# Closing the first expert list one unit earlier and moving the choices behind the unit's second scan

## The chip, the cores and the metric

The kernel runs on one core of a Trainium2 chip. The metric is device time in microseconds (us) of one execution, the median of several runs. Engines are named as in the profile: PE (matmuls), DVE (vector), ACT (scalar), POOL (indirect DMAs here), SP (the queue that issues most DMAs).

## What is computed

A gated recurrence over four sequences of 3648 steps, then a two-level mixture of experts over all 14592 rows. Cut to what matters:

```python
sig = 1.0 / (1.0 + np.exp(-f_logit))
f = lower_bound + (1.0 - lower_bound) * sig
for t in range(S):                                   # S = 3648, D = 256
    h = f[:, t] * h + (1.0 - f[:, t]) * x[:, t];  y[:, t] = h
x = y.reshape(B * S, D)                              # 14592 rows
g_idx = argmax(x @ w_group)                          # 4 groups
e_idx = argmax(x @ w_expert[g_idx])                  # 4 experts in each: 16 in all
out = g_w * e_w * (relu(x @ w1[g, e]) @ w2[g, e])    # w1 256x1024, w2 1024x256
```

The weights g_w and e_w are the two softmax values of the picked group and expert.

## The kernel before

**Phase one** walks over 29 units of 512 rows (the last has 256). For each unit it loads the gate and input (one 1 MB transfer `zt`), applies tanh and an affine map on ACT (L195, L205), multiplies on DVE (L241, later L221), runs two scans on DVE (L232, one for each half of the 256 features; the second is `p1_tb(u, 1)`), turns the result to row form with PE transposes (L259), computes router logits (L278, L291), and then **routes**: some thirteen small DVE instructions from `mx` (L301) to `posi` (L398) find each row's expert and its place in that expert's list; the count so far is kept in `runoff`, which ACT copies out of PSUM (L400). The rows are then scattered by POOL into the lists in HBM, one indirect DMA for each 128 rows (L361, `xs<-rows,posi`). Routing takes the units in groups: `GROUPS` says how many units are routed in one pass.

**Phase two** runs 32 jobs of two matrix products. Sixteen early jobs (A0 to A15) take the first 256 to 640 rows of a list before all rows are known; sixteen late ones (B0 to B15) take the rest in order of size, with at most `CAPS` rows each. `EARLY[i]` is, for early job i, the number of units after which its list is closed, and its length in 128-row tiles. `CHOOSE[i]` is the number of units after which its expert is picked, as the list that is fullest among those not yet taken (`choose`, L591 to L604 on DVE). A choice makes SP read the expert's number, write blank rows below the list, and start the expert's weight loads. When the list is closed, `place` (L615 to L622) fixes where the job's rows begin, and `early_rows` has SP load them (`xr<-xs`, L852), which waits for all scatters up to the cut. For A0 and A1 the weights are used as loaded, eight 256 KB pieces each (L867, matmuls L967 and L1002); later jobs load 512 KB pieces (L870) and split them on ACT and DVE (L878, L879).

The order on each engine is that of the code: phase one is a list of small steps (`p1_thunks`), and `bg_step` takes some of them after each step of phase two. `BEGIN` = 6 sets the mark "first": phase one runs alone up to it, then job A0 is entered. So PE, DVE and ACT each have one fixed sequence, with waits. Four `zt` buffers exist, so a unit's load waits until the unit four before it is scanned. SP's sequence is in code order too: a load that stands behind a wait on SP is issued after it.

In the code `u` is a unit number; in the step of unit u the unit u - 1 is routed. "After n units" is therefore the step u = n.

Of the kernel before, what the change touches and what calls it, by code (L numbers as in the profile page):

```python
# [19 lines left out]
NE = 16  # L20
UNIT = 512

EARLY = [(5, 2), (6, 2), (8, 2), (8, 2), (10, 3), (10, 3), (12, 3), (14, 3),
         (16, 4), (18, 4), (20, 4), (22, 5), (24, 5), (26, 5), (28, 5), (28, 5)]
CAPS = [972, 848, 808, 748, 536, 524, 516, 488, 448, 392, 340, 308, 240, 160, 144, 108]
EXTRA_AT = []
CHOOSE = [4, 5, 6, 6, 8, 8, 10, 12, 14, 16, 18, 20, 22, 24, 26, 26]
GROUPS = [1] * 6 + [2] * 11 + [1]
LAG = 7
FAST = 9  # L30
PLAN = []
ROWS_AT = {5: 6, 6: 7}
USED = float(1 << 22)
STG_BUFS = 8
RAW = 2
# [6 lines left out]
BEGIN = 6  # L42
# [6 lines left out]
def gated_scan_moe(ctx: ExitStack, tc, zx, lower, wroute, wexp, out, S):  # L49
# [7 lines left out]
    NT = N // P  # L57
    PRE = max(n for _, n in EARLY) * P
    LW = PRE + N + 2 * P
# [47 lines left out]
    nc.gpsimd.tensor_scalar(out=least, in0=eoff, scalar1=-16.0, scalar2=16.0, op0=ALU.mult, op1=ALU.add)  # L107
    cuts = {u for u, _ in EARLY}
    eidx = iota_f32("eidx", [NE], [[1, NE]])
# [297 lines left out]
    def p1_thunks(us, groups, parts):  # L407
# [21 lines left out]
        def put(f):  # L429
            th.append(f or (lambda: None))  # L430
            if hasattr(f, "mark"):
                marks[f.mark] = len(th)
# [11 lines left out]
        def wave(u, n):  # L444
            while parts and n and parts[0][0] <= u:
                put(parts.pop(0)[1])
                n -= 1
# [13 lines left out]
        for u in us + [us[-1] + 1]:  # L461
            seq = []
            if u <= FAST:
# [31 lines left out]
                elif u > 7:  # L495
                    wave(u, 1)
                    back(u - 1)
                for m in [m for m, v in ROWS_AT.items() if u == v]:
                    f = lambda m=m: early_rows(m)
                    f.mark = m  # L500
                    put(f)
                if u in cuts and u - 1 in ends:
                    put(lambda u=u: place(u))
                if u - 1 in ends:
                    put(lambda u=u: choose(u))
                put(lambda u=u: p1_tb(u, 1))
                wave(u, 1 if u < FAST else 99)
                if u == BEGIN:
                    f = lambda: None
                    f.mark = "first"  # L510
                    put(f)
                if u == FAST:
                    f = lambda: None
                    f.mark = "begun"
                    put(f)
                    for v in [v for v in sorted(cuts) if v <= FAST and v not in ROWS_AT]:
                        f = lambda v=v: early_rows(v)
# [16 lines left out]
            for t in seq:  # L534
                put(t)
                slot += 1
                for _ in range(1):
                    if not hold:
                        break
                    f = hold.popleft()  # L540
# [6 lines left out]
            if u - 1 in ends:  # L547
# [15 lines left out]
                if u in cuts:  # L563
                    rs.append(lambda u=u: place(u))
                    f = lambda u=u: early_rows(u)
# [10 lines left out]
        f = lambda: order()  # L576
# [673 lines left out]
```

## Time and profile before

| | |
|---|---|
| median of 3 runs | 781.66 us (780.29 to 782.87) |
| the profiled execution | 782.74 us |
| its span in the trace | 781.0 us |
| PE busy | 722.8 us (93%) |
| DVE busy | 536.1 us (69%) |
| ACT busy | 453.4 us (58%) |
| POOL busy | 293.5 us (38%) |

The span is what the instructions cover; the profiled execution's own time is 1.74 us longer. Busy shares are means over stages that differ, so the stages are read one by one.

### The profile page before, as it was taken

The page shows a single profiled execution, that of the slowest core. Times are in us where ns is not written, and L with a number is a line of the kernel's source. Part 1 is how long each engine was busy: PE and PEld are TensorE (multiplying, and loading weights), DVE is VectorE, ACT ScalarE, POOL GpSimd, SP SyncE. Part 2 cuts the span into 40 slices and gives each one's busy share as a digit, 9 for nine tenths or more (in the row PEclk, how much of TensorE's full clock was granted, in tenths as well). Part 3 has the DMA queues.
Part 4 walks back from the last instruction along what each step waited for, and adds up shares of the span by engine and source line. Part 5 has one row for each costly group of instructions (what it writes and reads, how often), then busy time and mean ns, then how long its engine had stood idle before and what let it go on. Part 6 is the DMA issues. An engine that isn't in the chain of part 4 may idle for free.

```text
span 781.0 us, 21520 instructions
## 1 busy us (share of the span) xinstructions
PE 722.8 (93%) x8182; PEld 641.8 (82%) x8182; DVE 536.1 (69%) x1154; ACT 453.4 (58%) x825; POOL 293.5 (38%) x272
## 2 busy tenths in 40 slices
PE   3666878999999999999999999999999999999995
PEld 1454657888888878998999989899999999999895
DVE  6885829999999996679456645554554656657661
ACT  5654827878878776454445544444454555556552
POOL 3641406858664764452221222222222231223222
PEclk9997979999999999999999999999999999999998
DMA  7798678998899875548857662334253555466530
GB/s 274 247 312 279 241 255 311 319 318 270 306 318 311 276 222 161 154 127 263 200 152 155 142 165 93 94 115 105 94 137 108 167 141 165 128 188 197 165 86 29
DMA packets 101963, 152.03 MB, mean 195 GB/s; under 512 B 60969, under 2 KB 70984, under 8 KB 98529
## 3 DMA queue, kind: packets, MB, share of 16 engines
q1 hardware_dynamic: 87328, 103.27, 46.5%
q0 software_dynamic: 11408, 30.02, 10.7%
q10 hardware_dynamic: 3120, 17.34, 6.4%
q8 instruction: 65, 1.06, 0.6%
q14 instruction: 42, 0.34, 0.2%
HBM read 112.66 MB, written 38.40 MB: 193 GB/s over the span
## 4 chain that ended last, share of the span: by engine, by line
PE 67%; DVE 16%; DMA 6%; issue 5%; ACT 3%; POOL 1%; SPq 1%; POOLq 0%; DVEq 0%; ACTq 0%
PE ps_m L1019 30%; PE ps_m L989 7%; PE ps_m L990 7%; PE ps_m L991 7%; DVE h L232 4%; DVE wl L879 3%; PE ps_p L989 3%; PE ps_p L990 3%; PE ps_p L991 3%; DVE hl L995 2%; DMA xs<-rows,posi 2%; PE ps_m L967 2%; PE ps_p L259 2%; DMA xr<-xs 2%; DMA xs<-blank 1%
## 5 line engine op out<-in xcount | busy, mean ns | idle before, releaser
L1019 PE MATMUL ps_m<-wh,hh 128*128 128x256 f16 (+3 forms) x1256 | 254.7, 251 | 1.2 <-ACT o L1031 1.2
L1019 PE MATMUL ps_m<-wh,hl 128*128 128x256 f16 (+3 forms) x1256 | 254.9, 251 | 0.1
L1019 PE MATMUL ps_m<-wl,hh 128*128 128x256 bf16 (+3 forms) x1256 | 254.7, 251 | 0.0
L1019 PEld LDWEIGHTS <-hh 128*128 128x128 f16 (+3 forms) x2512 | 186.3, 99 | 23.0 <-issue 4.5
L989 PE MATMUL ps_m<-xh,wh 128*128 128x256 f16 (+12 forms) x798 | 191.8, 255 | 6.0 <-DVE hl L995 5.5
L990 PE MATMUL ps_m<-xl,wh 128*128 128x256 bf16 (+12 forms) x798 | 192.0, 255 | 0.0
L991 PE MATMUL ps_m<-xh,wl 128*128 128x256 f16 (+12 forms) x798 | 191.9, 255 | 0.0
L879 DVE TENSOR_TENSOR wl<-st,wh 128x1024 bf16<-128x1024 f32 x120 | 144.7, 1218 | 57.3 <-ACT wh L878 57.3
L361 POOL DMA_INDIRECT xs<-rows,posi x114 | 139.3, 1222 | 116.5 <-ACT runoff L400 27.5
L1032 POOL DMA_INDIRECT out_dram<-o,info x71 | 82.9, 1167 | 235.2 <-ACT o L1031 203.2
L995 DVE SCALAR_TENSOR_TENSOR hl<-ps_m,hh 128x512 bf16<-128x512 f32 (+10 forms) x170 | 112.6, 666 | 61.2 <-ACT hh L994 60.9
L994 ACT ACTIVATE hh<-ps_m 128x512 f16<-128x512 f32 (+10 forms) x170 | 99.6, 589 | 66.8 <-PE ps_m L991 65.1
L878 ACT CAST wh<-st 128x1024 f16<-128x1024 f32 x120 | 124.3, 1049 | 14.1 <-PE ps_m L1019 8.7
L990 PEld LDWEIGHTS <-wh 128*128 128x128 f16 x1104 | 108.3, 98 | 12.9 <-issue 5.7
L989 PEld LDWEIGHTS <-wh 128*128 128x128 f16 x1104 | 108.2, 98 | 8.7 <-issue 1.0
L991 PEld LDWEIGHTS <-wl 128*128 128x128 bf16 x1104 | 108.2, 98 | 7.0
L1019 PEld LDWEIGHTS <-hl 128*128 128x128 bf16 (+3 forms) x1256 | 99.3, 99 | 10.0 <-issue 0.4
L1032 POOL DMA_INDIRECT out_dram<-o,meta x53 | 62.2, 1173 | 108.2 <-ACT o L1031 86.0
L1031 ACT ACTIVATE o<-ps_m,info 128x256 f32<-128x256 f32 (+4 forms) x71 | 31.5, 445 | 75.9 <-PE ps_m L1019 68.5
L989 PE MATMUL ps_p<-xh,wh 128*128 128x256 f16 (+17 forms) x306 | 71.5, 249 | 0.0
L991 PE MATMUL ps_p<-xh,wl 128*128 128x256 f16 (+17 forms) x306 | 71.4, 249 | 0.0
L990 PE MATMUL ps_p<-xl,wh 128*128 128x256 bf16 (+17 forms) x306 | 71.4, 249 | 0.0
(183 smaller groups left out, 840.7 us busy)
## 6 DMA issues: line engine op xcount, KB each, us to landing
st<-in_wexp_dram SPq DMA_DIRECT2D x120, 512.0 KB, 6.5
zt<-in_zx_dram ACTq DMA_DIRECT2D x16, 1024.0 KB, 8.4
zt<-in_zx_dram SPq DMA_DIRECT2D x10, 1024.0 KB, 10.1
xs<-blank SPq DMA_DIRECT2D x28, 258.0 KB, 10.0
xr<-xs SPq DMA_DIRECT2D x14, 258.0 KB, 4.1
wh<-in_wexp_dram SPq DMA_DIRECT2D x8, 256.0 KB, 5.8
wl<-in_wexp_dram SPq DMA_DIRECT2D x8, 256.0 KB
xs<-rows,posi POOLq DMA_INDIRECT x114, 6.1
```

The source lines that it names most:

```text
L232: nc.vector.tensor_tensor_scan(out=h[:, k, c0 - a:c1 - a], data0=ff[:, k, c0 - a:c1 - a], data1=uu[:, k, c0 - a:c1 - a], initial=init, op0 ...
L361: sc = nc.gpsimd.indirect_dma_start(out=xs_v[G["t0"] + t][:, :], out_offset=bass.IndirectOffsetOnAxis(ap=R["posi"][:, t:t + 1], axis=0), i ...
L878: nc.scalar.copy(j.wh[i], j.st[i])
L879: nc.vector.tensor_tensor(out=j.wl[i], in0=j.st[i], in1=j.wh[i], op=ALU.subtract)
L989: nc.tensor.matmul(po, w1_at(j.wh, k, c), xh[:, k], start=(k == 0), stop=False)
L990: nc.tensor.matmul(po, w1_at(j.wh, k, c), xl[:, k], start=False, stop=False)
L991: nc.tensor.matmul(po, w1_at(j.wl, k, c), xh[:, k], start=False, stop=(k == KD - 1))
L994: nc.scalar.activation(hi, pv, AF.Relu)
L995: nc.vector.scalar_tensor_tensor(out=j.hl[ch][:, cs[0]:cs[-1] + 1, 0:w], in0=pv, scalar=0.0, in1=hi, op0=ALU.max, op1=ALU.subtract)
L1019: nc.tensor.matmul(pm[i * q:i * q + n, 0:dw], h[ch][:, c, ts], w2_at(w, c)[:, i * dw:(i + 1) * dw], start=(c == 0 and s == 0), stop=(c == ...
L1031: nc.scalar.activation(o[s, 0:dw], pm[s, 0:dw], AF.Copy, scale=lt.bitcast(F32)[s, r, 1:2])
L1032: nc.gpsimd.indirect_dma_start(out=out_v[out_n[0]].rearrange("n (g d) -> (n g) d", g=g), out_offset=bass.IndirectOffsetOnAxis(ap=lt[s, r, ...
```

## The change

The first list is closed after four units (before: five) and its expert chosen after three (before: four); the second expert is chosen after four (before: five). The steps `place` and `choose` stand behind the unit's second scan (before: ahead of it), and the mark "first" ahead of that scan. Eight units are routed singly (before: six), then pairs. Job A0's rows are loaded in the step of unit 5 (before: 6), A1's in that of unit 7 as before. B0 may take 988 rows (before: 972).

```diff
-EARLY = [(5, 2), (6, 2), (8, 2), (8, 2), (10, 3), (10, 3), (12, 3), (14, 3),
+EARLY = [(4, 2), (6, 2), (8, 2), (8, 2), (10, 3), (10, 3), (12, 3), (14, 3),
-CAPS = [972, 848, 808, 748, 536, 524, 516, 488, 448, 392, 340, 308, 240, 160, 144, 108]
+CAPS = [988, 848, 808, 748, 536, 524, 516, 488, 448, 392, 340, 308, 240, 160, 144, 108]
-CHOOSE = [4, 5, 6, 6, 8, 8, 10, 12, 14, 16, 18, 20, 22, 24, 26, 26]
-GROUPS = [1] * 6 + [2] * 11 + [1]
+CHOOSE = [3, 4, 6, 6, 8, 8, 10, 12, 14, 16, 18, 20, 22, 24, 26, 26]
+GROUPS = [1] * 8 + [2] * 10 + [1]
-ROWS_AT = {5: 6, 6: 7}
+ROWS_AT = {4: 5, 6: 7}
...
+                if u == BEGIN:
+                    f = lambda: None
+                    f.mark = "first"
+                    put(f)
+                put(lambda u=u: p1_tb(u, 1))
+                wave(u, 1 if u < FAST else 99)
                 if u in cuts and u - 1 in ends:
                     put(lambda u=u: place(u))
                 if u - 1 in ends:
                     put(lambda u=u: choose(u))
-                put(lambda u=u: p1_tb(u, 1))
-                wave(u, 1 if u < FAST else 99)
-                if u == BEGIN:
-                    f = lambda: None
-                    f.mark = "first"
-                    put(f)
```

On DVE, the first choice of the kernel before stands between the end of a routing pass (`posi`) and the second scan of unit 4 (L232):

```order
L398 TENSOR_REDUCE posi<-sc 128x4
L591 SCALAR_TENSOR_TENSOR fill<-runoff,least 128x16
L593 MAX top<-fill 128x8
L595 MAX_INDEX who<-top,fill 128x8
L603 TENSOR_SCALAR sel<-fill,top 128x16
L604 SCALAR_TENSOR_TENSOR least<-sel,least 128x16
L232 SCALAR_TENSOR_TENSOR h<-zt,h 128x512
L241 SCALAR_TENSOR_TENSOR zt<-zt 128x1024
```

In the changed kernel the first choice comes one unit earlier, in the step of unit 3, and on DVE stands there as follows:

```order
L398 TENSOR_REDUCE posi<-sc 128x4
L232 SCALAR_TENSOR_TENSOR h<-zt,h 128x512
L591 SCALAR_TENSOR_TENSOR fill<-runoff,least 128x16
L593 MAX top<-fill 128x8
L595 MAX_INDEX who<-top,fill 128x8
L603 TENSOR_SCALAR sel<-fill,top 128x16
L604 SCALAR_TENSOR_TENSOR least<-sel,least 128x16
L241 SCALAR_TENSOR_TENSOR zt<-zt 128x1024
```

The scan has moved ahead of the choice, whose five rows now stand ahead of the next unit's multiplication (L241).

On SP, the start of the program (`zt` loads of whole units, then the first read of a chosen expert's number `who`), as a difference:

```order
 L183 DMA zt<-in_zx_dram 128x2x512 x2
-L185 DMA zt<-in_zx_dram 128x2048 x6
+L185 DMA zt<-in_zx_dram 128x2048 x5
 L597 TENSOR_LOAD who
 L597 ISA x2
```

One unit's load (that of unit 7) has moved behind the first choice and A0's eight weight loads. Likewise unit 8's load now stands behind A1's eight, and unit 9's behind A0's rows.

On DVE behind A0's entry, the kernel before routes units 6 and 7 in one pass of eight tiles (160 = 8 tiles of 20 logits), with a weight split (L879) between its rows:

```order
L232 SCALAR_TENSOR_TENSOR h<-zt,h 128x512 x2
L241 SCALAR_TENSOR_TENSOR zt<-zt 128x1024
L879 TENSOR_TENSOR wl_1238<-st,wh_1237 128x1024
L301 TENSOR_REDUCE mx<-Lg 128x40
L303 TENSOR_TENSOR ge<-Lg,mx 128x160
L232 SCALAR_TENSOR_TENSOR h<-zt,h 128x512
L307 SCALAR_TENSOR_TENSOR pw<-ge,pri 128x160
```

The changed kernel there has unit 8's multiplication and scans, and a pass for unit 6 alone; the pass for unit 7 begins behind unit 9's multiplication:

```order
L241 SCALAR_TENSOR_TENSOR zt<-zt 128x1024
L232 SCALAR_TENSOR_TENSOR h<-zt,h 128x512
L301 TENSOR_REDUCE mx<-Lg 128x20
L232 SCALAR_TENSOR_TENSOR h<-zt,h 128x512
L303 TENSOR_TENSOR ge<-Lg,mx 128x80
L307 SCALAR_TENSOR_TENSOR pw<-ge,pri 128x80
...
L398 TENSOR_REDUCE posi<-sc 128x4
L241 SCALAR_TENSOR_TENSOR zt<-zt 128x1024
L301 TENSOR_REDUCE mx<-Lg 128x20
```

One pass over eight tiles has become two passes over four, and the multiplication and two scans of unit 8, which stood ahead of A0's entry, stand behind it.

## Rows read from the trace of the kernel before

**Rows 1.** Busy time by stretch: PE, PEld, DVE, ACT, POOL, clock share, DMA share, GB/s.

```profile
40.00:44.00 4.00, 2.34 (x20) 1.62 (x21) 3.77 (x9) 2.50 (x6) 1.67 (x2) 1.00 0.76 139
44.00:64.00 20.00, 10.73 (x111) 8.97 (x109) 17.53 (x51) 8.89 (x20) 9.81 (x8) 0.95 1.03 377
...
66.00:75.00 9.00, 8.98 (x55) 6.09 (x56) 1.44 (x2) 5.21 (x12) 0.00 (x0) 0.66 0.73 210
...
103.00:113.00 10.00, 9.85 (x48) 7.60 (x48) 1.09 (x3) 2.08 (x5) 0.00 (x0) 0.67 0.79 252
...
140.00:300.00 160.00, 156.61 (x1648) 138.41 (x1646) 156.34 (x330) 126.34 (x239) 102.88 (x81) 1.00 0.89 288
300.00:781.00 481.00, 470.54 (x5809) 429.47 (x5806) 279.85 (x554) 243.18 (x419) 134.11 (x118) 0.99 0.52 140
```

**Rows 2.** PE in order of time: start, duration, work, idle before it and what ended that.

```profile
66.02 0.46 PE L933 MATMUL ps_p<-ident,xr 128*128 128x128 f32 x1 [8.02 <-DMA xr<-xs]
...
93.74 0.60 PE L967 MATMUL ps_m<-xl,wl 128*128 128x256 f32 x2
102.78 0.46 PE L933 MATMUL ps_p<-ident,xr 128*128 128x128 f32 x1 [8.44 <-DMA xr<-xs]
```

**Rows 3.** The chain of waits: start, duration, what.

```profile
50.92 7.25 DMA xs<-rows,posi
...
58.41 7.48 DMA xr<-xs
...
94.54 5.74 DMA xs<-rows,posi
...
101.18 2.17 DMA xr<-xs
```

**Rows 4.** DVE in order of time: a second scan, the first choice, a routing pass, the second choice.

```profile
29.49 1.27 DVE L232 TENSOR_TENSOR_SCAN h<-zt,h 128x512 f32<-128x512 f32 x1
...
37.68 0.17 DVE L591 SCALAR_TENSOR_TENSOR fill<-runoff,least 128x16 f32<-128x16 f32 x1 [1.66 <-ACT runoff L400]
...
38.18 0.17 DVE L595 FIND_INDEX8 who<-top,fill 128x8 uint32<-128x16 f32 x1
...
42.27 0.21 DVE L301 TENSOR_REDUCE mx<-Lg 128x20 f32<-128x80 f32 x1
...
44.95 0.22 DVE L398 TENSOR_REDUCE posi<-sc 128x4 int32<-128x64 f32 x1
46.76 0.18 DVE L615 SCALAR_TENSOR_TENSOR posA<-runoff,taken 128x16 int32<-128x16 f32 x1 [1.59 <-ACT runoff L400]
...
47.98 0.17 DVE L595 FIND_INDEX8 who<-top,fill 128x8 uint32<-128x16 f32 x1
```

**Rows 5.** ACT in order of time: the count of three units; unit 9's tanh.

```profile
30.96 0.18 ACT L400 COPY runoff<-ps_p 128x16 f32<-128x16 f32 x1
...
65.56 1.06 ACT L195 ACTIVATE zt<-zt 128x1024 f32<-128x1024 f32 x1 [7.42 <-DMA zt<-in_zx_dram]
```

**Rows 6.** SP's issues in order of time: loads of units 2 to 7, first blank, unit 9's load.

```profile
4.74 26.43 SPq L185 DMA_DIRECT2D zt<-in_zx_dram  x6
39.54 0.37 SPq L600 DMA_DIRECT2D xs<-blank  x1
...
55.72 0.80 SPq L185 DMA_DIRECT2D zt<-in_zx_dram  x1
```

**Rows 7.** DVE in order of time, later: four scans ahead of A0; units 6 and 7.

```profile
60.73 4.01 DVE L232 TENSOR_TENSOR_SCAN h<-zt,h 128x512 f32<-128x512 f32 x4
...
84.26 0.29 DVE L398 TENSOR_REDUCE posi<-sc 128x8 int32<-128x128 f32 x1
```

**Rows 8.** POOL: the first of the eight scatters of units 6 and 7.

```profile
85.32 0.97 POOL L361 DMA_INDIRECT xs<-rows,posi  x1 [22.53 <-ACT runoff L400]
```

**Rows 9.** PE at full rate: two following matmuls of 256 columns.

```profile
140.06 0.27 PE L990 MATMUL ps_m<-xl,wh 128*128 128x256 bf16 x1
140.17 0.27 PE L991 MATMUL ps_m<-xh,wl 128*128 128x256 f16 x1
```

## The prediction

> **What bounds the kernel now.** I read the busy time by stretch first, to split the run into stages, then the chain of waits for the start, then each engine in order of time around the gaps that the chain shows. From 140 us on PE is busy 156.6 of 160 us and then 470.5 of 481 [rows 1], and two matmuls of 256 columns follow each other at 0.11 us [rows 9], which is 2.4 GHz: nothing is to be won there by an earlier start of anything but the stage itself, and whatever arrives earlier at 140 us arrives earlier at the end. DVE is as full as PE up to 300 us (156.3 of 160), but its work behind A2's entry is the same in both kernels and in the same order, so it shifts too. The loss is ahead of that. PE does its first matmul for job A0 at 66.02, after 8.02 us of idle time; it runs out of A0 and A1 at 94.34 and waits 8.44 us for A2's rows, until 102.78 [rows 2]. Both times what ends the wait is a load of rows out of the lists, `xr`, which itself waits for the last scatter of the unit that closes the list: 50.92 to 58.17 to 65.89 for A0, 94.54 to 100.28 to 103.35 for the end of A2's loads [rows 3]. After both waits the clock stands at its lower level for a while: 0.66 over 66 to 75 and 0.67 over 103 to 113 [rows 1] mean about 6.1 and 6.6 us at 1.2 GHz.
>
> **The change: A0's start.** The first choice hangs on the count `runoff`. Before, DVE waits for it 1.66 us, then chooses; the number `who` is there at 38.35 [rows 4] and SP issues the blank rows at 39.54 [rows 6], the weights behind it. In the changed kernel the choice uses the count of three units, which ACT has at 31.14 [rows 5], and stands behind the scan that ends at 30.76 [rows 4]. With 0.1 us from the count to the choice and the same 0.67 to `who` as before (37.68 to 38.35 [rows 4]), `who` is there at 31.9: 6.5 us earlier. The five rows of a choice take about 1 us (0.67 and two more of some 0.2) and the wait behind the scan is some 0.5 us, so unit 4's multiplication and all behind it start 1.5 us later than before; this pushes unit 3's routing, but unit 4's second scan no longer waits for a count. The second choice, with a `place` ahead of it (46.76 to 48.15 for both until `who`), then ends at about 40.5 instead of 48.15: 7.6 us earlier.
>
> From the second `who` to A0's rows it took 17.7 us before (48.15 to 65.89). In it lie A1's eight weight pieces, one unit's `zt` (issued at 55.72) and the rows, while the DMA share is 1.03 at 377 GB/s [rows 1]. The same set follows the second choice now: eight pieces, then unit 8's `zt`, then A0's rows. The scatters that the rows wait for are one unit older: they come about 7.6 us earlier as well (the counts of two following units are 9.1 us apart, 37.68 against 46.76, less the 1.5 above), and they are not what lands last. So A0's rows land at 58.3 and PE starts there at 58.4. ACT's tanh ahead of A0's copies waits for unit 8's `zt` in place of unit 9's, which took 9.84 us from issue (55.72) to use (65.56) [rows 5, 6], so it moves along. **Term one: -7.6 us.** Its bounds: the first choice alone (-6.5) is inside; the 8.1 MB that flow from 40 to 64 us (139 GB/s for 4 us, 377 for 20 [rows 1]) would take 21.5 us at 377 GB/s without a gap, in place of 24 (-10), and 28.1 us at the 288 GB/s of 140 to 300 us (-3.5).
>
> All of this puts 2 MB of weights ahead of transfers that phase one needs. With SP's loads and POOL's scatters under way together the DMA share is at its full 1.03 [rows 1]. The Trainium skill (DMA: Bandwidth & Descriptors, Issuing engines are not separate DMA queues) says that DMAs of all issuing engines run on the same 16 engines and interleave; by that rule alone, the set of transfers from the first choice to A0's rows is one stream whose end moves as its start does, by 6.5 us and not 7.6, and the whole would come to 773.1. I take 7.6, because the stretch that receives the weights, 31 to 40 us, holds waits of SP for the scans (its six loads were drawn out over 26.4 us [rows 6]), and at 40 to 44 us the share was still 0.76 [rows 1].
>
> **From A0's start to A2's rows.** Before: 66.02 to 102.78, 36.76 us. It is 18.24 to the start of `posi` of units 6 and 7 [rows 7], 1.06 to the first scatter [rows 8], 9.22 to the eighth at 94.54 (seven steps of 1.32), 5.74 to its landing, 2.5 to PE. Now unit 6's scatters are issued by themselves, earlier, and behind unit 7's `posi` stand four: 3.95 in place of 9.22, a gain of 5.3. Against it DVE has more to do ahead of that `posi`: two passes over four tiles (2.9 us each, 42.27 to 45.17 [rows 4]) in place of one over eight, so up to 2.9 us more, and unit 8's multiplication and two scans (about 3.6), which before ran while A0's rows were awaited (four scans from 60.73 [rows 7]). Of these 6.5 us some fall into idle time: DVE was busy 1.44 of the 9 us from 66 [rows 1]. PE, too, now meets unit 6's and unit 7's count matmuls between A0's and must wait for DVE there. I let somewhat less than half of it lengthen the path, 2.9 us. **Term two: -5.3 + 2.9 = -2.4 us**, 34.4 us from A0 to A2. Bounds: -5.3 if all of it hides, +1.2 if none does.
>
> PE's own work between the two is 28.3 us (66.02 to 94.34), less about 3 if the clock stays up after A0's shorter wait, plus those waits; so PE still waits some 5 us for A2, against 8.44. Whether the clock falls in such a wait no row tells; I count it as falling: **term three, 0**, bound -3.3 (half of 6.6 us).
>
> **The rest.** B0's last chunk is 220 instead of 204 columns: 8 chunks of F x 2 halves x 3 products = 48 matmuls of 16 more columns at 0.11 us for 256 [rows 9], **+0.3 us**; all else of B0 keeps its number of tiles. Counted from the reference's routing of its own inputs, the first list has 238 rows after four units and 327 after five; A0 runs its 256 columns either way, so its cost is the same, and 18 rows more go to B0: 981 of 988. The two choices and two places are as many as before. The keep-warm matmuls of unit 5 move to unit 4, where PE is idle.
>
> **The sum.** -7.6 - 2.4 + 0 + 0.3 = -9.7 us. The profiled execution took 782.74 us for a span of 781.0, and 1.08 us more than the median; the difference applies to each alike: 781.66 - 9.7 = 772.0.
>
> **Rivals.**
> *The waits shrink further and the clock stays up.* Unit 6's pass lies wholly in DVE's idle time and A2's rows come before PE has been idle long enough to fall to 1.2 GHz. For it: 7.6 us of idle DVE right behind A0. Against it: DVE's rows there wait for logits that PE makes behind A0's first transposes. It gives -7.6 - 5.3 - 3.3 + 0.3 = -15.9, 765.8; with the bound of term one it would be 762.
>
> *Transfers eat the gain.* Weights, `zt` and rows of A2's list crowd into a shorter time: from 0 to 103 us the same bytes would have to flow in 93 us, and the blank rows of the third choice must land before A2's rows may be read. Then A0 starts only 3.5 us earlier and A2's path gains up to 2.4: 776 to 778.5. For it: a share of 1.03 for 20 us. Against it: 0.73 and 0.79 in the stretches after both waits.
>
> *It does nothing.* A0's rows stay behind unit 8's `zt` and A2's behind unit 7, and PE only waits longer at the second place for what it won at the first: 780 to 783. Against it: the path from A0 to A2 is tied to A0's start, since unit 6's logits stand behind A0's first transposes on PE.
>
> *Slower: unit 7's load comes too late.* Its SP issue was inside the first 26.4 us [rows 6], by 31.2; now it stands behind the first choice and eight weight pieces, at about 38.4. ACT takes its tanh one unit behind the second choice, near 49, in sequence and ahead of the copies that unit 5's routing needs, so each us of lateness costs a us. Behind full weight traffic unit 9's load took 9.84 us; that gives 48.2, just in time. It must land later than about 60 before it outweighs 9.7 us and the kernel becomes measurably slower than before; 22 us for 1 MB is twice what any row shows. At 25 us the time would be 785.
>
> **Numbers.** Forecast, 769 to 775: 0.48. Waits shrink further, 762 to 769: 0.24. Transfers eat it, 775 to 779.3: 0.19. Nothing, within 2.3 us of 781.66 (0.3%, about what a measurement of this kernel tells from no change): 0.05. Slower: 0.04. So faster 0.91. The range 765 to 778.5 leaves out the ends of the second and third case and the last two, some 0.19.
>
> **What would show it.** In the profile after: first `who` at about 32, second at 40.5; PE's first L933 near 58.4; four scatters between unit 7's `posi` and A2's rows, PE's second wait for `xr` ending near 93; the clock at 0.66 or higher behind it; the same rows as before from there, about 10 us earlier. I am wrong if the first L933 is later than 62, if ACT waits long for `zt` of unit 7, if DVE is full from A0 to A2 and `posi` comes later than 23 us behind A0, or if PE shows new waits between 110 and 300 us that the earlier start uncovers.

## The result, and the profile after

The changed kernel takes 771.46 us (median of four runs, 766.36 to 771.74), the kernel before 781.03 on the same chip (four runs, 780.29 to 782.87). The ratio is 0.9859, with a 95% interval of 0.9814 to 0.9903: faster, clear of the noise, by about 11 us if one goes by the ratio and by 9.57 if by the medians. The forecast was 772.0, in a range of 765 to 778.5. The profiled execution after took 771.69 us, for a span of 769.8; the profiled one before, 782.74 for 781.0. The rows below are read against each other on those two, 11.2 us apart in span. Ratios and comparisons leave out the runs in which the chip was in a slower state. From here on the engines go by their names: TensorE is PE (PEld its weight loads), VectorE DVE, ScalarE ACT, GpSimd POOL, and SyncE the queue SP.

One thing about the order of work has to be known for what follows. The kernel lays down the order of TensorE, VectorE and ScalarE as the code has it only up to A0's entry (`manual_schedule`, L1152). Behind it the order is fixed too, but it is not that of the code: A0's second product (L1002, 32 matmuls in the trace, 16 for each of its two row tiles) is issued in the code behind all of A1's first product (L967), and in the trace a part of it runs ahead of A1's transposes, 14 of the 32 before and 20 after. So an edit can also move rows that it does not name.

VectorE after, in order of time: the first and the second choice, and `posi` of unit 7.

```profile
31.50 0.17 DVE L595 FIND_INDEX8 who<-top,fill 128x8 uint32<-128x16 f32 x1
...
40.12 0.17 DVE L595 FIND_INDEX8 who<-top,fill 128x8 uint32<-128x16 f32 x1
...
77.79 0.19 DVE L398 TENSOR_REDUCE posi<-sc 128x4 int32<-128x64 f32 x1
```

The second `who`, at 48.15 before [rows 4], ends at 40.29. The first one ends at 31.67.

TensorE after: the stand-in matmuls ahead of A0, A0's first transposes (L933), the last product ahead of the wait for A2, A2's transposes, and the next count (L384).

```profile
54.23 4.20 PE L268 MATMUL ps_m<-upto,tri 128*128 128x128 bf16 x44
58.50 0.36 PE L933 MATMUL ps_p<-ident,xr 128*128 128x128 f32 x1
...
88.93 0.60 PE L967 MATMUL ps_m<-xl,wl 128*128 128x256 f32 x2
93.48 0.46 PE L933 MATMUL ps_p<-ident,xr 128*128 128x128 f32 x1 [3.95 <-DMA xr<-xs]
95.05 0.92 PE L933 MATMUL ps_p<-ident,xr 128*128 128x128 f32 x3 [1.12 <-DMA xr<-xs]
...
101.99 0.23 PE L384 MATMUL ps_p<-oh16f,upto 128*128 128x128 bf16 x1
```

The same count before, as a landmark for what lies behind A2's entry:

```profile
113.86 0.23 PE L384 MATMUL ps_p<-oh16f,upto 128*128 128x128 bf16 x1
```

A0 starts at 58.50 in place of 66.02, and its wait of 8.02 us [rows 2] is gone. A2 starts at 93.48 in place of 102.78, after 3.95 and 1.12 us of waiting in place of 8.44. At the count the lead is 11.87 us (at the one after it, 131.39 against 119.52, too), so 2.57 us more were won between A2's entry and the count; of the 11.87, 11.2 are left at the end.

SyncE's queue after: A0's rows, the next blank rows (which wait for those to land), A2's rows.

```profile
51.73 0.90 SPq L852 DMA_DIRECT2D xr<-xs  x2
...
58.81 1.50 SPq L600 DMA_DIRECT2D xs<-blank  x2
...
88.68 3.04 SPq L852 DMA_DIRECT2D xr<-xs  x4
```

ScalarE after: the tanh of unit 8, which waited for that unit's load, and in its queue, at the same time as A2's rows, the load of a later unit.

```profile
58.03 1.06 ACT L195 ACTIVATE zt<-zt 128x1024 f32<-128x1024 f32 x1 [2.81 <-DMA zt<-in_zx_dram]
...
88.70 0.36 ACTq L185 DMA_DIRECT2D zt<-in_zx_dram  x1
```

GpSimd after: the first and the last of the four scatters of unit 7.

```profile
79.65 0.97 POOL L361 DMA_INDIRECT xs<-rows,posi  x1 [6.70 <-ACT runoff L400]
...
83.48 1.03 POOL L361 DMA_INDIRECT xs<-rows,posi  x1 [0.30 <-issue]
```

The chain of waits after: unit 8's load, and at A2's rows, in place of 5.74 and 2.17 [rows 3], the last scatter and the rows.

```profile
49.81 8.20 DMA zt<-in_zx_dram
...
83.48 4.87 DMA xs<-rows,posi
89.25 5.76 DMA xr<-xs
```

Ahead of A2 the chain before ran through A0's rows (58.41 to 65.89 [rows 3]) and TensorE. After, it does not touch them: it runs through unit 8's load (49.81 to 58.01), ScalarE's tanh and VectorE to unit 7's scatters.

Busy time by stretch after (columns as in [rows 1]): ahead of A0, nine us from A0's start, the stretch of [rows 1] behind A0, from A2's entry to the next count, and the full stage.

```profile
44.00:58.00 14.00, 10.01 (x85) 8.57 (x85) 12.86 (x42) 7.42 (x17) 5.97 (x8) 0.52 1.04 379
58.50:67.50 9.00, 6.92 (x64) 5.12 (x65) 5.91 (x17) 6.81 (x16) 1.85 (x2) 1.00 0.99 272
66.00:75.00 9.00, 8.96 (x58) 7.20 (x57) 7.46 (x17) 8.15 (x16) 4.13 (x4) 1.00 1.01 400
...
93.48:101.99 8.51, 7.39 (x42) 5.38 (x43) 1.83 (x4) 1.64 (x5) 0.00 (x0) 0.70 1.00 355
...
140.00:300.00 160.00, 156.28 (x1628) 137.69 (x1626) 152.23 (x339) 122.58 (x233) 104.00 (x78) 1.00 0.84 275
```

And the same stretch before, from A2's entry to the next count:

```profile
102.78:113.86 11.08, 10.93 (x53) 8.16 (x53) 1.09 (x3) 2.17 (x5) 0.00 (x0) 0.69 0.80 257
```

The clock is at 1.00 over 66 to 75 in place of 0.66 [rows 1]. It has been low earlier instead: 0.52 over 44 to 58, where TensorE had stood idle for 3.12 us ahead of 44.77 and where most of the stand-ins ran (44 in 4.20 us, at a share of 0.61; before, 44 in 2.62 us at 1.00). The full stage is as it was: 156.28 of 160 us busy against 156.61.

### The profile page after: what moved, and what is told of

It reads as the page before. It is cut to its first block, busy times and chain, and to the rows that moved or that the text cites. A ratio compares the mean times of both kernels' runs of the same rounds, so it can differ in the third digit from the quotient of the medians.

```text
span 769.8 us, 21533 instructions
## 1 busy us (share of the span) xinstructions
PE 720.2 (94%) x8179; PEld 640.4 (83%) x8179; DVE 537.2 (70%) x1166; ACT 453.3 (59%) x827; POOL 296.7 (39%) x272
## 3 DMA queue, kind: packets, MB, share of 16 engines
q8 instruction: 64, 1.05, 0.6%
## 4 chain that ended last, share of the span: by engine, by line
PE 64%; DVE 12%; DMA 9%; issue 6%; ACT 5%; POOL 2%; SPq 1%; POOLq 0%; ACTq 0%; DVEq 0%
PE ps_m L1019 30%; PE ps_m L989 7%; PE ps_m L990 7%; PE ps_m L991 7%; DMA xs<-rows,posi 4%; PE ps_p L989 3%; PE ps_p L991 3%; PE ps_p L990 3%; DVE h L232 3%; DVE wl L879 2%; DMA zt<-in_zx_dram 2%; PE ps_p L259 2%; DMA xs<-blank 2%; POOL out_dram L1032 1%; DVE hl L995 1%
## 5 line engine op out<-in xcount | busy, mean ns | idle before, releaser
L1019 PE MATMUL ps_m<-wh,hh 128*128 128x256 f16 (+3 forms) x1256 | 254.7, 251 | 1.5 <-ACT o L1031 1.5
L1019 PE MATMUL ps_m<-wh,hl 128*128 128x256 f16 (+3 forms) x1256 | 254.9, 251 | 0.1
L1019 PE MATMUL ps_m<-wl,hh 128*128 128x256 bf16 (+3 forms) x1256 | 254.6, 251 | 0.0
L1019 PEld LDWEIGHTS <-hh 128*128 128x128 f16 (+3 forms) x2512 | 186.3, 99 | 23.3 <-issue 4.8
L361 POOL DMA_INDIRECT xs<-rows,posi x114 | 144.2, 1265 | 104.4 <-issue 28.6
L879 DVE TENSOR_TENSOR wl<-st,wh 128x1024 bf16<-128x1024 f32 x120 | 144.6, 1218 | 51.5 <-ACT wh L878 51.0
L1019 PEld LDWEIGHTS <-hl 128*128 128x128 bf16 (+3 forms) x1256 | 99.3, 99 | 10.0 <-issue 0.4
L1032 POOL DMA_INDIRECT out_dram<-o,meta x53 | 60.6, 1143 | 106.1 <-ACT o L1031 87.0
```

Source lines behind the costliest of these rows:

```text
L361: sc = nc.gpsimd.indirect_dma_start(out=xs_v[G["t0"] + t][:, :], out_offset=bass.IndirectOffsetOnAxis(ap=R["posi"][:, t:t + 1], axis=0), i ...
L879: nc.vector.tensor_tensor(out=j.wl[i], in0=j.st[i], in1=j.wh[i], op=ALU.subtract)
L1019: nc.tensor.matmul(pm[i * q:i * q + n, 0:dw], h[ch][:, c, ts], w2_at(w, c)[:, i * dw:(i + 1) * dw], start=(c == 0 and s == 0), stop=(c == ...
L1032: nc.gpsimd.indirect_dma_start(out=out_v[out_n[0]].rearrange("n (g d) -> (n g) d", g=g), out_offset=bass.IndirectOffsetOnAxis(ap=lt[s, r, ...
```

## The experiments

The kernels ran on three chips, named A, B and C here: the kernel before takes 836.94, 824.64 and 824.57 us on them, so that none gives the 781.03 of the first result, whose chip is not on record (it is called the first chip below). Their traces show waits that the first one's do not, such as one of 3.20 us on ScalarE that is put down to another core or an unknown queue (the page's "remote"), and TensorE's weight loads for the long products (L1019) wait 11 to 18 us in all on "issue" in place of 4.8. So ratios are to the kernel before on the same chip, and of the traces the part up to A2 is read, where events come some 1 us later than on the first chip. In kernels with added lines, L941 is L933, L1010 is L1002 and L389 is L384. Medians in us; intervals of 95%. The whole change ran on B and C only. Where two kernels of one chip are set against each other directly, the means of their runs are compared (5 to 12 runs each), with a 95% interval.

| kernel | chip | median | before | ratio |
|---|---|---|---|---|
| e1_pairs: lists alone | A | 828.73 | 836.94 | 0.9917 (0.9881 to 0.9953) |
| e2_singles_only: singles alone | A | 830.24 | 836.94 | 0.9922 (0.9887 to 0.9957) |
| e3_choice_ahead | A | 831.75 | 836.94 | 0.9933 (0.9894 to 0.9971) |
| e4_second_late | A | 833.55 | 836.94 | 0.9949 (0.9919 to 0.9978) |
| c1_control: the whole change | B | 816.07 | 824.64 | 0.9913 (0.9880 to 0.9947) |
| e5_warm_both | B | 812.66 | 824.64 | 0.9878 (0.9828 to 0.9928) |
| e6_warm_a2 | B | 812.76 | 824.64 | 0.9890 (0.9833 to 0.9947) |
| e8_all | B | 821.87 | 824.64 | 0.9954 (0.9914 to 0.9995) |
| c2_control: the whole change | C | 815.71 | 824.57 | 0.9893 (0.9839 to 0.9947) |
| e1_again: lists alone | C | 818.39 | 824.57 | 0.9925 (0.9891 to 0.9960) |
| e2_again: singles alone | C | 820.95 | 824.57 | 0.9944 (0.9905 to 0.9983) |
| e9_before_warm_a2 | C | 830.42 | 824.57 | 1.0065 (1.0027 to 1.0103) |

### The two halves

The theory is that of the prediction: the earlier lists bring A0's start forward, the single routing shortens the way from A0 to A2. The rival is that one half does all, or that each alone wins what both do.

The changed kernel with units 6 and 7 routed as a pair again (lists alone):

```diff
-GROUPS = [1] * 8 + [2] * 10 + [1]
+GROUPS = [1] * 6 + [2] * 11 + [1]
```

> The changed kernel with six units routed singly, then pairs, as before; choices, cut and their place as changed. Theory (earlier choices bring A0's entry forward, single routing shortens the way from A0 to A2): first who still near 31.6, A0's first L933 still at 58 to 59, but eight scatters behind the pass of units 6 and 7, so A2's first L933 moves from 93.5 to 95.5 to 98; time 773.5 to 776. Rival (A2's rows hang on the routing of unit 7 alone, and A0's entry is worth nothing): A2 back at 102, time 780.

> The early choice and the later place of the choice alone; units 6 and 7 routed as a pair again. Theory, by the prediction's terms and the first trace of this kernel: the first entry comes 6 to 7.6 us earlier and the way from it to the third block is that of before or 0 to 2 us shorter; at the third block 6 to 8 us are won, and the end keeps them: 0.990 to 0.992 of before. The halves add up: this gain and that of the singles alone make that of the whole change (0.986 to 0.988 together). Rival: each half alone wins what both win (0.991, 0.992 and 0.991 were measured, in two calls), because something behind the third block sets the end from a certain point on; then the control is not more than 1 us ahead of this kernel.

The kernel before with eight units routed singly (singles alone):

```diff
-GROUPS = [1] * 6 + [2] * 11 + [1]
+GROUPS = [1] * 8 + [2] * 10 + [1]
```

> The kernel before with eight units routed singly, nothing else. Theory: A0's entry stays at 66, the way from there to A2 shortens from 36.8 to 32 to 34.5 us, so A2's first L933 at 98 to 100.5 and the time 776.5 to 779. Rival (single routing is the whole gain): 772. Rival (the second pass costs DVE as much as it saves): 780 to 782.

> Eight units routed singly alone, with the lists and the place of the choice as before. Theory: entry of the first block as before, the way from it to the third block 4 to 5 us shorter, 0.993 to 0.996 of before, and the control ahead of it by 4 us or more. Rival: as said for the other half, level with the control within 1 us.

The whole change, unaltered, beside them:

> The changed kernel itself, unaltered, so that the ratios of the experiments beside it can be set against its own on the same chip. Expected 0.986 of the kernel before (its first result, 0.9814 to 0.9903); if the chip has the extra stalls on TensorE and ScalarE that the first four experiments showed, 0.988 to 0.993.

> The changed kernel itself once more, beside its two halves and a kernel on its clock, all on one chip: the fourth corner of a square (before, lists alone, singles alone, both). Expected 0.986 to 0.991.

TensorE in the lists alone (e1_again): A0's and A2's first transposes.

```profile
60.77 0.36 PE L933 MATMUL ps_p<-ident,xr 128*128 128x128 f32 x1 [1.64 <-DMA xr<-xs]
...
99.28 0.63 PE L933 MATMUL ps_p<-ident,xr 128*128 128x128 f32 x4
```

The same in the singles alone (e2_again):

```profile
65.56 0.46 PE L933 MATMUL ps_p<-ident,xr 128*128 128x128 f32 x1 [7.01 <-DMA xr<-xs]
...
99.17 0.64 PE L933 MATMUL ps_p<-ident,xr 128*128 128x128 f32 x4
```

And in the whole change on that chip (c2_control):

```profile
60.05 0.36 PE L933 MATMUL ps_p<-ident,xr 128*128 128x128 f32 x1 [1.64 <-DMA xr<-xs]
...
93.26 0.63 PE L933 MATMUL ps_p<-ident,xr 128*128 128x128 f32 x4
```

The last scatter of unit 7 on GpSimd in the lists alone (e1_again):

```profile
89.71 0.98 POOL L361 DMA_INDIRECT xs<-rows,posi  x1 [0.30 <-issue]
```

The same scatter in the singles alone (e2_again):

```profile
89.96 1.12 POOL L361 DMA_INDIRECT xs<-rows,posi  x1 [0.31 <-issue]
```

A0's start follows the lists: 60.77 with them, 65.56 without, and the wait there, 7.01 us, stays with the old lists. The way from A0 to the last scatter follows the routing: 28.94 us with a pair (89.71 - 60.77), 24.40 with singles (89.96 - 65.56). The first pair of traces, on chip A, says the same: A0 at 60.17 and 66.52, and 29.87 and 24.10 us from there to the last scatter. On the first chip it was 28.52 before (66.02 [rows 2] to 94.54 [rows 3]) and 24.98 after. Each half does its own part, and that is shown. TensorE's entry into A2 shows less, because none of the three waits for rows there: on these chips its own work ahead of A2 ends later. Over the 8 us ahead of A2 the clock was 1.00 in c2_control and 0.57 in e1_again, where TensorE had first stood idle 4.80 us on "issue".

By time, each half is faster than before on both chips, by about what was expected: the lists 0.9917 on A and 0.9925 on C (0.990 to 0.994 and 0.990 to 0.992 expected), the singles 0.9922 and 0.9944 (0.994 to 0.997 and 0.993 to 0.996); where the median lies outside the range, the interval reaches into it. On C the gains are 0.0075 and 0.0056 for the halves and 0.0107 for the whole. Compared directly, the whole is 4.1 us (0.4 to 7.8) in front of the singles alone and 3.4 us (-0.3 to 7.1) in front of the lists alone. A sum of the two gains, 0.0131, and the rival's "no more than the better half" both lie inside the intervals, so the times alone do not settle whether the halves add up.

Behind A2's entry the same kernels show something that the prediction did not count. Busy time by stretch, from A2's entry to the next count, in the lists alone (e1_again):

```profile
99.28:104.72 5.44, 5.44 (x43) 4.34 (x42) 4.67 (x10) 4.67 (x11) 0.00 (x0) 1.00 0.99 365
```

The same stretch in the singles alone (e2_again):

```profile
99.17:106.79 7.62, 7.62 (x54) 6.18 (x52) 5.10 (x11) 5.49 (x11) 0.00 (x0) 1.00 0.99 360
```

And in the whole change (c2_control):

```profile
93.26:98.71 5.45, 5.45 (x44) 4.35 (x42) 5.31 (x11) 4.77 (x11) 0.00 (x0) 1.00 0.98 314
```

At full clock and without a wait this stretch is 54 matmuls and 7.62 us with the old lists, 43 or 44 and 5.45 us with the new ones: ten more matmuls of A0's second product (L1002) stand ahead of A2 there. Before, 16 of its 32 lie behind A2's entry, after, 6; all traces with the old lists and without added stand-ins have 16, those with the new ones 6 (e4_second_late none). Before, at 0.69, the 53 matmuls that the trace holds took 11.08 us; after, at 0.70, 42 took 8.51 with 1.12 of waiting.

That they are A0's and not A1's shows on the first chip before, in a row of TensorE and in the row of ScalarE that writes the last part of what A1's second product reads:

```profile
110.94 0.59 PE L1002 MATMUL ps_m<-wh,hl 128*128 128x256 f32 x2
...
112.49 0.60 ACT L970 ACTIVATE hl<-ps_m 128x512 f32<-128x512 f32 x1
```

The products with `hl` begin at 110.94, ahead of A1's `hl` at 112.49. A0's last `hl` was written at 80.29 to 80.91. So before, while TensorE waited 8.44 us for A2's rows, 16 matmuls (3.5 us at the full clock) whose inputs had long been written stood behind the wait in its order. No run moved only them.

### Where the choice stands, and when the second one comes

The changed kernel with `place` and `choose` ahead of the unit's second scan:

```diff
+                if u in cuts and u - 1 in ends:
+                    put(lambda u=u: place(u))
+                if u - 1 in ends:
+                    put(lambda u=u: choose(u))
                 if u == BEGIN:
...
                 wave(u, 1 if u < FAST else 99)
-                if u in cuts and u - 1 in ends:
-                    put(lambda u=u: place(u))
-                if u - 1 in ends:
-                    put(lambda u=u: choose(u))
```

> The changed kernel with place and choose ahead of the second scan again. Theory (what counts is that the choices come one unit earlier; behind the scan each saves about 1.1 us of the chain): first who still near 31.6, second who 41.4 instead of 40.3, A0's entry 1 to 1.5 us later, time 772.5 to 773.5. Rival (the place behind the scan is the main part): 776 or more.

The blank rows of the second list are issued at 44.08 there, 1.9 us later than in e1_pairs on the same chip (42.16), and TensorE's 44 stand-ins run only from 58.38 (55.26 there); A0 starts at 61.34, against 60.17. So the place behind the scan is worth about 1.2 us at A0's start, in one trace of each, as the theory said (1 to 1.5). The time does not confirm it: the theory's 772.5 to 773.5 is 0.988 to 0.990, the rival's 776 or more 0.993 or more; 0.9933 lies with the rival, its interval holds both, and the whole change, against which it would have to be set, did not run on A.

The changed kernel with the second list chosen at five units, as before:

```diff
-CHOOSE = [3, 4, 6, 6, 8, 8, 10, 12, 14, 16, 18, 20, 22, 24, 26, 26]
+CHOOSE = [3, 5, 6, 6, 8, 8, 10, 12, 14, 16, 18, 20, 22, 24, 26, 26]
```

> The changed kernel with the second expert chosen after five units, as before, so that its 2 MB of weights come behind A0's rows on SP. Theory (A0's rows and unit 8's input end a stream of transfers behind the second choice): without A1's weights ahead, A0's rows land near 53 and unit 8's tanh starts 3 to 5 us earlier; PE itself reaches A0 at 58 at the earliest, since its keep-warm matmuls end there, so A0's entry gains at most 1 us and A2's 1 to 3; time 768.5 to 771. Rival (PE's own sequence sets the entry and DMA is no part of it): 771.5. Rival (A1's weights now come too late): PE waits ahead of A1's first L967 and the time is 774 or more.

SyncE's queue in e4_second_late: A0's rows, the blank rows that wait for them, A1's rows.

```profile
50.24 0.91 SPq L852 DMA_DIRECT2D xr<-xs  x2
54.21 0.36 SPq L600 DMA_DIRECT2D xs<-blank  x1
...
70.93 0.94 SPq L852 DMA_DIRECT2D xr<-xs  x2
```

TensorE in e4_second_late: the stand-ins, in two parts, and the first transposes of A0 and A1.

```profile
55.30 2.30 PE L268 MATMUL ps_m<-upto,tri 128*128 128x128 bf16 x22
57.44 0.70 PE L933 MATMUL ps_p<-ident,xr 128*128 128x128 f32 x4
...
69.12 1.39 PE L268 MATMUL ps_m<-upto,tri 128*128 128x128 bf16 x22
...
80.66 0.38 PE L933 MATMUL ps_p<-ident,xr 128*128 128x128 f32 x1 [1.46 <-DMA xr<-xs]
```

The rows of A0 have landed by 54.21, where A1's weights no longer flow ahead of them, but TensorE comes to them only at 57.44: its own sequence is the next bound, 2.7 us ahead of the 60.17 of e1_pairs on that chip. That sequence is not the same, though: 22 of the 44 stand-ins, those of A1, have moved behind A0's entry, and the 22 that are left take 2.30 us where the 44 took 4.29 in e1_pairs, so some 2 of the 2.7 us can come from that. And A1 now waits 1.46 us for its rows. The time is a miss: 768.5 to 771 (0.983 to 0.986) were expected, 0.9949 was measured, which is in the range of the second rival (774 or more, 0.990), though the wait stands at A1's rows and not at its weights. What costs the time was not followed; the entry into A2 does not show it (94.84, against 94.65 in c1_control on another chip).

### The clock, ahead of A0 and at A2

Stand-ins (`keep_warm`, matmuls whose result is not used) at units 4 and 5, in the changed kernel:

```diff
-        if 2 <= u <= EARLY[0][0]:
+        if 2 <= u <= 5:
...
-            if G["t0"] * P == EARLY[0][0] * UNIT:
+            if G["t0"] * P in (4 * UNIT, 5 * UNIT):
```

> The changed kernel with its stand-in matmuls kept both at unit 4 and at unit 5 (and six behind each early router up to unit 5). Theory: the first entry at 58.50 us is set by TensorE's own sequence, whose 44 stand-in matmuls ran at 1.2 GHz from 54.23 to 58.43, because the granted clock fell at 43.9 us when the stand-ins moved to unit 4. With stand-ins at both places the clock stays at 1.00 from 44 to 58, the 44 take about 2.6 us instead of 4.2, and the entry is then met by the landing of the rows (58.5 to 58.8 us by SyncE's next blank): entry within 0.5 us of before, the time 0 to 1.5 us shorter than the changed kernel's own. Rival: the clock falls there all the same, since the idle stretch ahead of unit 5's counting is what lowers it; then 1.5 us longer for the added matmuls, entry at 60.

TensorE in e5_warm_both: the stand-ins and A0's first transposes.

```profile
55.45 3.02 PE L268 MATMUL ps_m<-upto,tri 128*128 128x128 bf16 x44
59.78 0.36 PE L933 MATMUL ps_p<-ident,xr 128*128 128x128 f32 x1 [1.31 <-DMA xr<-xs]
```

A0 starts at 59.78 after waiting 1.31 us for its rows, in c1_control on that chip at 59.99 after 0.57. The landing sets it, as the theory said. But the clock did not stay up as it said: it was 0.68 over 44 to 58, in place of the control's 0.62, and the 44 took 3.02 us. So what a full clock there would do at A0 was not tested. The median is 3.4 us under the control's; the intervals of the ratios overlap (0.9828 to 0.9928 and 0.9880 to 0.9947), and compared directly it is 3.0 us (0.5 to 5.5) faster, in 6 runs. If that is a gain, A0's start is not its cause.

The changed kernel with 60 stand-ins ahead of A2's transposes, and the kernel before with 130:

```diff
+    def keep_warm_late(pm, n):
+        for _ in range(n):
+            tc.keep_in_program_order(nc.tensor.matmul(pm[:, UNIT - P:UNIT], tri, upto, start=True, stop=True))
...
+        if j.kind == "A" and j.idx == 2:
+            pm = bank("m2")
+            keep_warm_late(pm, 60)     # 130 in the kernel before
```

> The changed kernel with 60 stand-in matmuls just ahead of the third block's first transposes, where TensorE waited 3.95 and 1.12 us for the rows from 89.5 on. Theory: they fill the wait (60 at some 55 ns are 3.3 us), the granted clock does not fall from 91.8 to 98.5, and the rows from 95 to 103 run at 1.00 instead of 0.78: about 9 us at 0.5 to 0.6 give back 1.5 to 2.5 us, if TensorE sets the pace behind the wait. Rival: VectorE and ScalarE set it there (the score's scan waited 4.63 us for TensorE's counting, which argues against), and the time stays within 0.5 us of the changed kernel's.

> The kernel before with 130 stand-in matmuls just ahead of the third block's first transposes, where TensorE waited 8.44 us for rows (94.34 to 102.78) and then worked some 8 us at the lower clock (0.67 over 103 to 113). The lists, the routing and the transfers are those of before. Theory (the third term was no zero): the clock stays up, the entry stays at 102.8 or comes up to 0.5 us later, the transposes and products behind it take 4 us instead of 8, and the kernel is 2 to 4 us shorter, a ratio of 0.995 to 0.9975. Of that the changed kernel got about half, since its own lower stretch behind the third block's entry was 5 us instead of 8. Rival: another engine sets the pace there and nothing is won (0.999 to 1.001), or the 130 matmuls run past the landing and cost (1.001 to 1.003).

TensorE in e9_before_warm_a2, from the row that ScalarE's wait delayed to A2's transposes:

```profile
97.72 0.66 PE L259 MATMUL ps_p<-ident,h 128*128 128x128 f32 x4 [4.08 <-ACT Lg L297]
...
103.28 7.42 PE L273 MATMUL ps_m<-upto,tri 128*128 128x128 bf16 x130
110.54 0.69 PE L941 MATMUL ps_p<-ident,xr 128*128 128x128 f32 x4
```

ScalarE in e9_before_warm_a2: the wait that delayed it.

```profile
95.25 0.60 ACT L978 ACTIVATE hh<-ps_m 128x512 f32<-128x512 f32 x1 [3.20 <-remote]
```

e9 is slower than before, by 0.0027 to 0.0103, and the theory's 0.995 to 0.9975 is a miss. TensorE came to the stand-ins at 103.3, not at 94.3 as on the first chip; A2's rows were issued at 97.90 and had landed when the stand-ins ended, so all or most of their 7.42 us stood on the path to A2 instead of in a wait. It does not test what the clock costs behind a wait. e6 is a miss of the same kind: its control met A2 without a wait on that chip (94.65), so there was nothing to fill; 60 stand-ins took 3.51 us and A2 began at 95.17. Its median is 3.3 us under the control's, which cannot be told from nothing (3.2 us, -1.4 to 7.7, compared directly).

Neither run changes the stand-ins alone. They write to `bank("m2")`, the buffer that the second products use, and in e6, e8_all and e9 not one of the 32 matmuls of A0's second product stands ahead of A2's transposes, where the changed kernel has 26 there and the kernel before 16. That A2 began only 0.5 us later in e6 than in its control hides 5.6 us of work that moved behind it (26 at 0.216 us), and the 0.0065 of e9 is the price of the stand-ins together with such a move.

All three together (both sets of stand-ins and the second choice at five units):

> Both sets of stand-ins, and the second list chosen at unit 5 instead of 4. Theory: the choice at unit 5 puts the first block's transfer ahead, so its rows land at about 54 us, and with the clock kept up TensorE comes to the first transposes at about 56.5: entry 2 us earlier than the changed kernel's 58.50, of which the third block's entry sees up to 1.5; with the clock kept behind the third block's wait another 1.5 to 2.5 us. Together 2 to 4 us under the changed kernel: a ratio 0.003 to 0.005 under its own. Rival: the second list, chosen later, brings the second block's rows late (0.4 to 1.5 us of wait in the fourth experiment), which eats the gain: within 1 us.

TensorE in e8_all: the first transposes of A0 and A1, and the first matmuls of A0's second product.

```profile
57.18 0.67 PE L941 MATMUL ps_p<-ident,xr 128*128 128x128 f32 x4
...
80.75 0.46 PE L941 MATMUL ps_p<-ident,xr 128*128 128x128 f32 x1 [9.30 <-DMA xr<-xs]
...
101.50 1.03 PE L1010 MATMUL ps_m<-wh,hh 128*128 128x256 f32 x4
```

A0 starts 2.8 us earlier than in the control (57.18 against 59.99), and A1 waits 9.30 us for its rows until 80.75, where the control starts it at 79.05. The gain at A0 is gone at A1, as the rival said. But the time is worse than the rival's "within 1 us": compared directly, e8_all is 4.5 us (2.1 to 7.0) slower than the control. A1's rows come when they did in e4_second_late (80.66); there TensorE had all of A0's second product to do ahead of them (32 matmuls, 6.9 us at the full clock) and waited 1.46 us, here it stands behind A2, from 101.50 on. So the wait of 9.30 is for the most part work that the stand-ins' edit moved away, which no run separates from the later list. No version was found that is clearly faster than the changed kernel; e5_warm_both is at most a hint.

## Why the prediction was right, step by step

**Term one, A0's start: right.** -7.52 us (66.02 to 58.50) against -7.6. The first `who` ended at 31.67 (31.9 foretold), the second at 40.29 (40.5). The step "the same set of transfers follows the second choice" held: 17.9 us from `who` to TensorE's start before (48.15 to 66.02), 18.2 after. What the prediction did not see is that TensorE came to A0 only at 58.43, most of its stand-ins running at 1.2 GHz (a share of 0.50 up to 57, 0.61 over all 44); and SyncE's blank rows at 58.81 show that the rows had landed by then. With the rows early, TensorE's sequence sets the start (57.44 in e4_second_late, 57.18 in e8_all); with TensorE waiting, the rows do (e5_warm_both and the controls). That the start is met to 0.1 us is in part luck: two bounds fell together there. Unit 8's load moved along as foretold: ScalarE's tanh of it began at 58.03 in place of 65.56 (unit 9's, [rows 5]), 7.53 us earlier. It matters more than the prediction made of it, since the chain to A2 now runs through this load and not through A0's rows. The Trainium skill (DMA: Bandwidth & Descriptors, Issuing engines are not separate DMA queues) says that the DMAs of all issuing engines interleave on the same 16 engines. The figure that the prediction worked out from that, 6.5 us, is 1 us short of the row; the choice of 7.6 was the better one.

**Term two, from A0 to A2: right in sum, by two errors against each other.** 34.98 us against 34.4 foretold and 36.76 before: -1.78 in place of -2.4. From A0 to the last scatter it went better than foretold: -3.54 us (28.52 to 24.98) in place of -2.4, since `posi` of unit 7 came 19.3 us behind A0 and not 21.1, though the first scatter followed it after 1.86 us and not 1.06. "Somewhat less than half" of the 6.5 us of added VectorE work, 2.9, was too much: 1.05 us lengthened the path (18.24 to 19.29). In the nine us from A0's start VectorE is busy 5.91 us where it had been 1.44 [rows 1], so most of the added work went into idle time. From the last scatter to TensorE it went worse: 10.0 us (83.48 to 93.48) against 8.24 before, 1.76 given back: the scatter landed 0.87 us sooner (4.87 against 5.74), the rows came 2.63 us slower. SyncE issued them at 88.68 and ScalarE's queue a load of 1 MB at 88.70; they took 4.8 us to the first transposes, at a DMA share of 0.76, where before 2.17 us lay between (issued at 100.61, used at 102.78 [rows 2]), at 0.40. In c2_control ScalarE's load came 2.4 us behind the rows (92.59 against 90.15), and TensorE had them, without a wait, 3.1 us after their issue. That the two transfers share the engines fits all of these; no run moved the load alone, so the cause is argued, not shown.

**Term three, the clock: the mis-sized term.** "I count it as falling: term three, 0." The wait that it was to follow came out as foretold, 5.07 us for "some 5" (though the prediction did not size the waits among A0's and A1's matmuls that it took off for it). The clock did fall in A2's wait (0.70 from A2's entry to the next count, 0.69 before), but the stretch behind it became 2.57 us shorter. It divides, with the full-clock lengths of the two orders from e2_again and c2_control as a measure: 7.62 to 5.45, -2.17 us, for the ten matmuls of A0's second product that are now done ahead of A2; 11.08 - 7.62 = 3.46 of lower clock before and 8.51 - 1.12 - 5.45 = 1.94 after, -1.52; and the second wait of 1.12, +1.12 (0.15 before is inside the 3.46). So the term was about -1.5 from the clock and -2.2 from the order of the work, less 1.1 for the second wait; the prediction held the rows behind A2 to be the same. The lengths at full clock are from other chips; the division is an estimate from these rows, its sum is measured.

**The sum.** -7.52 - 1.78 - 2.57 = -11.87 at the next count, and +0.67 comes back by the end. Half of that is B0's 16 rows, for which +0.3 had been counted. GpSimd's rows that write the output show it, the second and the sixth of B0's, before:

```profile
466.38 0.97 POOL L1032 DMA_INDIRECT out_dram<-o,info  x1 [1.65 <-ACT o L1031]
...
486.35 0.97 POOL L1032 DMA_INDIRECT out_dram<-o,info  x1 [1.11 <-ACT o L1031]
```

and after:

```profile
454.68 0.97 POOL L1032 DMA_INDIRECT out_dram<-o,info  x1 [1.65 <-ACT o L1031]
...
474.97 0.97 POOL L1032 DMA_INDIRECT out_dram<-o,info  x1 [1.10 <-ACT o L1031]
```

The lead is 11.70 us at the one and 11.38 at the other, 0.32 less; the rest, some 0.2 us ahead of it and some 0.2 behind, was not followed. The prediction had -10.0 at A2 and -9.7 in all; the profiled executions differ by 11.05, the medians by 9.57. That the median meets 772.0 to 0.5 us is luck in part: in the traces term two won 0.6 us less than counted and term three 2.6 us more.

**The rivals.** *Waits shrink further*: in part. Most of the added VectorE work hid and about 1.5 of the 3.3 us of clock came, but not by the way it named, since the clock did fall. *Transfers eat the gain*: only the 2.63 us that A2's rows took longer. *It does nothing*: the path from A0 to A2 was tied to the moved transfers, and A2 came 9.3 us earlier. *Unit 7's load too late*: ScalarE's tanh of unit 7 at 48.97 shows no wait for it; SyncE's queue did stand from 45.22 to 48.20 among the weights of A1, 2.8 us of it for a `zt` load, and the profile's chain passes this by. *New waits behind 110*: none; the waits of TensorE there are those of the kernel before (0.56 and 1.20 us near 120, 0.57 and 1.20 near 132).

## What to carry to other kernels

A choice that comes 7.9 us earlier moved the whole stream of transfers behind it by nearly the same time here (7.5 us), and what follows is read from the next consumer: A0's rows, unit 8's load and TensorE's own sequence reached the same point within some 0.5 us, and a further advance has to move all of them, without making the next block's rows late (in e4_second_late and e8_all they were). Behind a wait count two things beside the wait: at which clock the next rows run, and which work the new order has already done ahead of it. Ask also whether work whose inputs are ready stands behind the wait: before, 16 matmuls did. Fill a wait with stand-ins only where the wait is sure to be there, and look at what else the edit moves; where the wait was gone, 130 of them took 7.42 us of TensorE, moved A0's second product behind A2, and the kernel was 0.0027 to 0.0103 slower.

## What was not expected of the hardware

The same kernel took 781 us in the first result and 824.6 to 836.9 on the three chips of the experiments. Its gain from this change was 0.0141 in the first and 0.0087 and 0.0107 on two of the chips; the intervals overlap, so a different gain is not shown. On these the waits on which the third term rests were not there, because TensorE's own work ahead of A2 ended later. The clock ahead of A0 differed too in kernels that hold the same order up to there: over 44 to 58 us it was 1.00 in e2_again and 0.63 in e9_before_warm_a2, on chip C. In e9 it stood at 0.50 from 44 to 54; why it had fallen there and not in e2_again is open.
